# mLSTM and MoE kernel: the decay matrix from an outer product on TensorE, the last unit by halves, one more row buffer, and a new order table

## Chip, core and metric

One core of a Trainium2 chip runs the whole program. The metric is the device time of one execution in microseconds (us), the median of several runs. Of the kernel before there are three runs: 322.81, 322.91 and 323.3 us.

## What is computed

An mLSTM layer (4 batches, 8 heads, 768 steps, head size 40) is followed by a mixture-of-experts style layer (3072 tokens of width 320, hidden width 1024). Cut to what matters:

```python
for t in range(S):                       # attention part, per batch and head
    m_new = max(f[t] + m, i[t])
    f_stab = exp(f[t] + m - m_new); i_stab = exp(i[t] - m_new); m = m_new
    C = f_stab * C + i_stab * outer(v[t], k[t])
    n = f_stab * n + i_stab * k[t]
    y[t] = sigmoid(o[t]) * (C @ q[t]) / max(|n . q[t]|, 1)
x = y as (3072, 320)
h = x @ w_in                             # 320 -> 1024
e = exp(h - max(h)); solu = h * e / (sum(e) + 1e-9)
out = layer_norm(solu) * g_ln @ w_out    # 1024 -> 320
```

## The kernel before

The recurrence is computed by chunks of 128 steps. A *unit* u is one batch and one chunk, 24 units in all (6 chunks of 4 batches, chunk by chunk). First the gates of all 32 rows (batch x head) are handled at once: `m` by a scan (L393), the log decay within the chunk G by two subtractions and a scan with resets at the chunk starts (L402 to L409), and `i - m - G` on POOL (L432, L440). G goes to DRAM as the tensor `gd` (L419), and PE transposes both into `bG` (L448 to L461).

A unit then goes through these steps (names are those of the trace):

- SP loads the tokens `tk` (484 KB, v, k and q, L803) and the row `gb`: G of 8 heads x 128 steps, copied to all 128 partitions (512 KB, L804).
- DVE takes the largest magnitude `am` (L829) and its reciprocal `rr`; ACT and DVE write q and k as two float16 parts into `qs` (L849, L857); SP transposes `qs` to `qT` by DMA (L873).
- POOL sets `gb` to -1e30 above the diagonal (L889); ACT computes the decay `d` = exp(gb + bG) with 8 instructions, one per head, because the bias is another column for each (L904).
- PE computes scores into a `sy` bank of PSUM (L946), DVE multiplies them by `am` and `d` into `p` (L958), PE multiplies `p` with the values (`intra`, L1008) and adds the part of the earlier chunks (`inter`, L982, scaled on DVE as `y`, L990). DVE normalises to `x` (L1026 to L1046), POOL multiplies by the output gate (L1058). `sy` has two banks, which all of these take in turn.
- For all chunks but the last, the state is updated: POOL makes `kt` (L926), PE the state's product `upd` into the bank `sx` (L1072), DVE and POOL the new state in bfloat16 parts `cs` and `c` (L1082 to L1116), and SP copies these (L1122, L1123).
- PE transposes `x` into `sx` (L1132); ACT and DVE write high and low parts (L1137 to L1151). The first product `ph` (L1185) has 16 matmuls of 128x512. Then the softmax and norm: DVE `nm` (L1201), ACT `e` (L1208), DVE `e` again (L1234), ACT `sq` (L1243), small DVE steps up to `ab` (L1254), POOL `pw` (L1262), DVE `so` (L1266).
- ACT and POOL write `e` as two float16 parts `us` (L1287, L1277), SP transposes these by DMA into a buffer `big` (L1282), and the second product (L1305, 24 matmuls of 128x320) uses the single PSUM bank `so_`. ACT scales it to `ot` (L1321), SP writes it out (L1326).

At the start the weights come in as float64 and are decoded on ACT and DVE (L523 to L558), w_out is centred and scaled (L679, L737), and the second product can't begin before that is done. While PE waits there it runs idle matmuls (L1340).

The order of the instructions on each engine is fixed when the program is built. `Plan` takes all operations with an assumed duration each, and a list scheduler picks the next one by a rank from the table `RANK` (three numbers per step: an offset in units, one that fades over the first four units, one that grows over the last four). Each engine and each DMA queue then works strictly in that order. One rule of `Plan` matters here: operations marked `mix=1` (the steps of `intra`) are woven with one marked `mix=2` (a quarter of the second product, 6 matmuls) where both are ready, so that their matmuls alternate:

```python
if self.mix[n]:
    c = [m for m in avail[eng] if self.mix[m] == 3 - self.mix[n] and ready[m] <= s]
    if c:
        m = min(c, key=lambda m: (ops[m][5], m))
        both.append(m)
```

Of the kernel before, what the change touches and what calls it, by code (L numbers as in the profile page):

```python
# [20 lines left out]
L = 128  # L21
# [23 lines left out]
BIG = 5  # L45
# [5 lines left out]
    "sp tk": (-22.15, -15.74, 11.02),  # L51
    "sp gb": (-18.49, -14.13, -3.91),
    "sp sg": (-12.92, -3.66, 10.34),
    "act sg": (10.97, -42.22, -5.32),
    "dve am": (64.38, -5.53, 8.99),
    "dve rr": (1.15, -13.23, -1.49),
    "act qs": (0.01, 0.34, -7.27),
    "dve qs": (27.98, -124.31, 34.38),
    "sp qT": (9.36, -8.48, -13.5),
    "act dec": (3.09, 0.05, 10.84),  # L60
    "pool gb": (-8.33, 9.33, 8.59),
    "act d": (3.59, 7.99, 4.76),
    "pool kt": (16.19, 14.15, -11.51),
    "pe ps": (1.88, -8.07, -14.15),
    "dve p": (13.14, -7.12, 9.09),
    "pe sy": (-25.21, -3.11, 0.05),
    "dve y": (-9.98, -11.72, 7.82),
    "dve rd": (-12.32, 2.97, -7.38),
    "dve yi": (-11.01, -10.07, 1.66),
    "dve x": (12.24, -2.05, 6.62),  # L70
    "pool x": (-1.85, -4.93, 7.89),
    "pe sx": (1.46, -15.56, -22.4),
    "pool ct": (31.71, -5.5, -11.21),
    "dve cs": (-7.83, -3.62, -5.53),
    "pool cs": (20.95, 2.35, -4.01),
    "pool c": (11.82, 9.23, -4.49),
    "sp cs": (-5.86, -3.37, -0.69),
    "act xh": (-4.75, -11.04, 11.47),
    "dve xl": (-3.73, 2.37, -17.47),
    "pe ph": (-8.01, -14.77, -2.96),  # L80
    "dve us": (-13.91, -14.09, -14.92),
    "dve s": (-16.7, 2.43, -7.18),
    "dve nm": (-9.34, 8.77, -1.66),
    "act e": (-5.06, -11.12, 5.47),
    "dve e": (2.3, 76.54, 6.54),
    "act sq": (3.67, 47.8, 13.39),
    "dve z": (57.44, 1.42, 6.82),
    "dve ab": (-11.07, 12.82, -11.55),
    "pool pw": (-4.81, -14.34, 0.96),
    "dve so": (6.71, -4.52, 4.73),  # L90
    "act us": (13.31, 30.02, -8.95),
    "pool us": (12.85, 4.2, -8.55),
    "sp big": (7.27, -12.21, -13.1),
    "pe so_": (15.47, 4.1, 6.95),
    "act ot": (14.85, -1.73, 0.39),
    "sp ot": (13.08, -5.34, 7.83),
    "sp w_in": (-51.81,),
    "sp w_out": (-2.36,),
    "w_in": (-2.99,),
    "w_out": (-14.05,),  # L100
    "w_mul": (-13.44,),
# [232 lines left out]
def mlstm_moe_kernel(ctx: ExitStack, tc: tile.TileContext, tok, og, fg, ig, w_in, w_out, gln, out):  # L334
# [70 lines left out]
    P.op(DVE, 3330, mk_g, [G1], [F_, M_], prio=g0, port=True)  # L405
# [10 lines left out]
    for b in range(B):  # L416
        load(
            300,
            lambda P, b=b: nc.sync.dma_start(  # L419
                out=P[("gd", 0)][b].rearrange("c h l -> h c l"),  # L420
                in_=gt(P, G_)[b * H : (b + 1) * H, :].rearrange("h (c l) -> h c l", l=L),
            ),
            [("gd", 0, b)],
            [G_],
            prio=g0,
        )


    P.op(
        POOL,  # L430
        1790,
        lambda P: nc.gpsimd.tensor_tensor(out=gt(P, I_), in0=gt(P, I_), in1=gt(P, M_), op=ALU.subtract),  # L432
        [I_],
        [M_],
        prio=g0,
    )
    P.op(
        POOL,
# [947 lines left out]
```

## Time and profile before

| | |
|---|---|
| median of three runs | 322.91 us |
| profiled execution, its own time | 324.31 us |
| its span, first to last instruction | 322.5 us |
| PE, DVE, ACT, POOL busy | 279.7, 264.3, 239.7, 174.5 us |
| bytes moved by DMA | 66.66 MB |
| first matmul of a second product | 85.5 us |

The lanes are PE (matmuls), PEld (weight loads of PE), DVE, ACT, POOL and SP, which issues all DMA transfers. A row of a stage table gives its start and end, its length, busy time of each lane with the number of instructions, then the granted TensorE clock (PEclk), the mean busy share of the 16 DMA engines, and GB/s. Busy time of PE is modelled and includes idle matmuls. In a chain or a timeline the first number is the start, the second the duration. A row of waits gives the waiting engine and line, what it waited for, the total, the number of times and the longest.

### The profile page before, as it was taken

What the parts mean: (1) busy time and instruction counts of PE and PEld (TensorE: products, weight loads), DVE (VectorE), ACT (ScalarE), POOL (GpSimd) and SP (SyncE); (2) the same over time, 40 slices, a digit from 0 to 9 for tenths busy, and PEclk for the clock granted to TensorE, in tenths of its full rate; (3) what the DMA queues carried; (4) which work ended last, traced back from release to release, by engine and by line L of the source; (5) the groups of instructions that cost most, each with busy time, mean ns of one, the idle gap of its engine ahead of it and who ended that gap; (6) DMA issues with size and microseconds to landing.
All of it is one profiled execution on the core that took longest, in us unless ns stands there. A gap on an engine that the chain in (4) does not pass through costs nothing.

```text
span 322.5 us, 6918 instructions
## 1 busy us (share of the span) xinstructions
PE 279.7 (87%) x2403; PEld 229.8 (71%) x2403; DVE 264.3 (82%) x671; ACT 239.7 (74%) x505; POOL 174.5 (54%) x186
## 2 busy tenths in 40 slices
PE   0189979697989999897999969999889989999984
PEld 0189868475868888686778848878767767888753
DVE  7978998999999888859969866988889889887740
ACT  2466788989788999649979847987869967635641
POOL 6435152638467847763848655666657655434210
PEclk9999988969999999999999997999999999999999
DMA  7599995899889999999989999999998999634391
GB/s 218 202 250 252 331 255 195 196 259 224 165 255 213 238 187 231 216 250 239 217 200 227 258 208 239 185 233 225 239 200 229 212 241 190 133 66 91 82 155 58
DMA packets 118723, 66.66 MB, mean 207 GB/s; under 512 B 102880, under 2 KB 110016, under 8 KB 118688
## 3 DMA queue, kind: packets, MB, share of 16 engines
q1 hardware_dynamic: 118688, 66.21, 89.0%
q8 instruction: 19, 0.31, 0.4%
q14 instruction: 16, 0.13, 0.2%
HBM read 33.85 MB, written 4.03 MB: 117 GB/s over the span
## 4 chain that ended last, share of the span: by engine, by line
PE 42%; DVE 14%; DMA 14%; issue 13%; POOL 9%; SPq 3%; ACT 3%; POOLq 0%; ACTq 0%; DVEq 0%
PE ph L1185 14%; DMA tk<-in_tok_dram 5%; PE sy L1008 4%; DMA gb<-gd 4%; PE sx L1132 2%; DMA big<-us 2%; POOL x L1058 2%; POOL gb L889 2%; PE sy L946 2%; PE sy L982 2%; PE sx L1072 1%; POOL us L1277 1%; DVE qs L857 1%; DMA out_dram<-ot 1%; DVE wg L547 1%
## 5 line engine op out<-in xcount | busy, mean ns | idle before, releaser
L1305 PEld LDWEIGHTS <-big 128*128 128x128 f16 x576 | 63.2, 118 | 18.0 <-DMA big<-us 3.8
L904 ACT ACTIVATE d<-gb,bG 128x128 f32<-128x128 f32 x192 | 59.0, 390 | 3.5 <-POOL gb L889 1.7
L1008 PEld LDWEIGHTS sy<-tk,p 128*128 128x128 f32 x384 | 57.4, 198 | 2.9 <-DVE p L958 0.3
L849 ACT ACTIVATE qs<-tk,rr 128x640 f16<-128x640 f32 x48 | 37.2, 819 | 26.7 <-DVE rr L842 23.2
L1008 PE MATMUL sy<-tk,p 128*128 128x41 f32 x384 | 56.6, 253 | 0.1
L1277 POOL TENSOR_TENSOR us<-e,us 128x1024 f16<-128x1024 f32 x23 | 49.1, 2139 | 11.0 <-ACT us L1287 10.8
L889 POOL TENSOR_SCALAR_AFFINE_SELECT gb<-gb 128x1024 f32<-128x1024 f32 x24 | 27.3, 1137 | 37.8 <-ACT dec L885 21.7
L829 DVE TENSOR_REDUCE am<-tk 128x1 f32<-128x640 f32 x24 | 19.5, 812 | 21.9 <-DMA tk<-in_tok_dram 21.9
L958 DVE SCALAR_TENSOR_TENSOR p<-sy,am,d 128x512 f32<-128x512 f32 x48 | 35.0, 736 | 2.4 <-PE sy L946 2.3
L1262 POOL TENSOR_TENSOR pw<-ab,mhalf 128x1 f32<-128x1 f32 x24 | 13.2, 551 | 42.4 <-DVE ab L1254 41.9
L1201 DVE TENSOR_REDUCE nm<-ph 128x1 f32<-128x1024 f32 x24 | 29.2, 1217 | 7.1 <-PE ph L1185 6.9
L1185 PE MATMUL ph<-wih,xh 128*128 128x512 f32 x96 | 34.1, 437 | 0.0
L1058 POOL TENSOR_TENSOR x<-x,sg 128x320 f32<-128x320 f32 x24 | 21.8, 908 | 20.3 <-DVE rr L842 7.8
L1243 ACT ACTIVATE sq<-e,nmean 128x1024 bf16<-128x1024 f32 x24 | 27.5, 1146 | 5.8 <-DVE e L1234 5.4
L1234 DVE SCALAR_TENSOR_TENSOR e<-ph,s,e 128x1024 f32<-128x1024 f32 x24 | 30.6, 1273 | 0.9 <-ACT e L1208 0.9
L1208 ACT ACTIVATE e<-ph,nm 128x1024 f32<-128x1024 f32 x24 | 26.6, 1109 | 5.0 <-DVE nm L1201 4.7
L1185 PE MATMUL ph<-wil,xh 128*128 128x512 f32 x96 | 30.1, 394 | 0.0
L857 DVE SCALAR_TENSOR_TENSOR qs<-tk,rr,qs 128x320 f16<-128x320 f32 x48 | 29.0, 633 | 0.5 <-ACT qs L849 0.3
L1287 ACT CAST us<-e 128x1024 f16<-128x1024 f32 x24 | 24.9, 1035 | 2.7 <-issue 2.6
L1185 PE MATMUL ph<-wih,xl 128*128 128x512 f32 x96 | 26.5, 398 | 0.2 <-DVE xl L1143 0.2
L926 POOL TENSOR_TENSOR kt<-tk,d 128x320 f32<-128x320 f32 x20 | 16.5, 829 | 11.9 <-ACT d L904 10.7
L1132 PE MATMUL sx<-ident,x 128*128 128x128 f32 (+1 forms) x72 | 12.8, 289 | 10.7 <-POOL x L1058 5.9
(181 smaller groups left out, 691.7 us busy)
## 6 DMA issues: line engine op xcount, KB each, us to landing
gb<-gd SPq DMA_DIRECT2D x24, 512.0 KB
tk<-in_tok_dram SPq DMA_DIRECT2D x24, 484.0 KB
sg<-in_og_dram SPq DMA_DIRECT2D x12, 320.0 KB
out_dram<-ot SPq DMA_DIRECT2D x24, 160.0 KB
big<-in_w_out_dram SPq DMA_DIRECT2D x4, 640.0 KB
cs<-cs SPq DMA_DIRECT2D x20, 102.5 KB
big<-in_w_in_dram SPq DMA_DIRECT2D x4, 512.0 KB
cs<-c SPq DMA_DIRECT2D x20, 51.2 KB
```

Source lines behind the costliest of these rows:

```text
L849: nc.scalar.activation(out=dst, in_=q_src(P, a).unsqueeze(2).to_broadcast([L, H, 2, D]), func=AF.Copy, scale=P[rr],)
L857: V.scalar_tensor_tensor(out=q_parts(P, a, 2 - a, 1), in0=q_src(P, a), scalar=P[rr], in1=q_parts(P, a, 0, 1), op0=ALU.mult, op1=ALU.subtract,)
L889: lambda P: nc.gpsimd.affine_select(out=P[gb], in_=P[gb], pattern=[[0, H], [1, L]], base=0, channel_multiplier=-1, compare_op=ALU.is_ge, f ...
L904: nc.scalar.activation(out=P[d_t][:, h, :], in_=P[gb][:, h, :], func=AF.Exp, bias=P[BG][:, 0, c, b * H + h : b * H + h + 1],)
L958: lambda P, j=j, ps=ps: V.scalar_tensor_tensor(out=P[p_t][:, 4 * j : 4 * j + 4, :], in0=P[ps].rearrange("p (h l) -> p h l", l=L), scalar=P ...
L1008: nc.tensor.matmul(yv(P)[:, h, :], lhsT=P[p_t][:, h, :], rhs=v1(P)[:, h, :], start=True, stop=True)
L1058: lambda P: nc.gpsimd.tensor_tensor(out=P[x], in0=P[x], in1=P[sg][:, u % OG, :], op=ALU.mult),
L1185: nc.tensor.matmul(P[ph][:, j * 512 : (j + 1) * 512], lhsT=a, rhs=w[:, j * 512 : (j + 1) * 512], start=n == 0, stop=n == 7,)
L1201: lambda P: V.tensor_reduce(out=P[nm], in_=P[ph], axis=AX.X, op=ALU.max, negate=True),
L1234: lambda P: V.scalar_tensor_tensor(out=P[e], in0=P[ph], scalar=P[sc], in1=P[e], op0=ALU.mult, op1=ALU.mult, accum_out=P[nmean]),
L1277: (V if last else nc.gpsimd).tensor_tensor(out=P[us[1]][:, 1], in0=P[e], in1=P[us[0]][:, 0], op=ALU.subtract)
L1305: nc.tensor.matmul(P[po][:, 0:DM], lhsT=uTv(P, a)[:, k, :], rhs=P[w][:, k, :], start=n == 0, stop=n == 23)
```

## The change

Seven things are done together.

1. The decay comes from TensorE. `i - m - G` (b) and G are split into two parts (rounded to the matmul format, and the rest) and go to DRAM as `bd` and `gd`. For each unit SP loads 16 rows of 128 into `el` (b's parts for 8 heads) and 2 x 8 x 128 into `er` (G's parts). Rows 0 and 1 of `el` are ones, the other rows of `er` say which head a row is for, the rest is zero. One matmul over all 128 rows makes the exponents of four heads in a `sy` bank; ACT takes exp of 512 columns at once (2 instructions in place of 8); POOL sets `d` to zero above the diagonal afterwards, in place of `gb` beforehand; DVE multiplies the scores into `d` itself, so that `p` is gone and `d` has 3 buffers.
2. The 512 KB load `gb` and the buffers `gb` and `p` are gone.
3. `kt` takes the last column of `d` from a small copy `dl` that ACT makes. The decay of the state comes for all units at once from one matmul at the start (`sel`, `dec`) in place of 16 small ACT steps.
4. The gates' steps on POOL move to DVE, and four small steps split the parts.
5. The state's product `upd` is marked `mix=1` with 8 steps: it may be woven into the second product.
6. The last unit goes by halves of 512 columns: first product, maximum, exp, multiplication, float16 parts, four transposes of half the size, second product by halves.
7. `BIG` is 6 in place of 5, and all numbers of `RANK` are others.

```diff
-BIG = 5
+BIG = 6
 RANK = {
-    "sp tk": (-22.15, -15.74, 11.02),
+    "sp tk": (-18.64, 10.68, -13.3),
...
-        load(1500, lambda P: nc.sync.dma_start(out=P[gb], in_=P[("gd", 0)][b, c].partition_broadcast(L)), [gb], [("gd", 0, b)], prio=rank(SPQ, "gb"))
+        load(
+            100,
+            lambda P: nc.sync.dma_start(
+                out=P[el].bitcast(F32)[2 : 2 + 2 * H],
+                in_=P[BD].rearrange("p a s -> (p a) s")[b * 2 * H : (b + 1) * 2 * H, c * L : (c + 1) * L],
+            ),
...
+        load(
+            100,
+            lambda P: nc.sync.dma_start(
+                out=P[er].bitcast(F32)[0:2],
+                in_=P[GD][b * H : (b + 1) * H, :, c * L : (c + 1) * L].rearrange("h a l -> a h l"),
+            ),
...
-        def decay(P, j):
-            for h in range(4 * j, 4 * j + 4):
-                nc.scalar.activation(
-                    out=P[d_t][:, h, :],
-                    in_=P[gb][:, h, :],
-                    func=AF.Exp,
-                    bias=P[BG][:, 0, c, b * H + h : b * H + h + 1],
-                )
+        for j in range(2):
+            pd = ("sy", ("d", u, j))
+
+            def exponents(P, j=j, pd=pd):
+                nc.tensor.matmul(
+                    P[pd],
+                    lhsT=P[el],
+                    rhs=P[er].rearrange("p h l -> p (h l)")[:, j * 512 : (j + 1) * 512],
+                    start=True,
+                    stop=True,
+                )
+
+            P.op(PE, 232, exponents, [pd], [el, er], rank(PE, "d"))
+            op(
+                ACT,
+                600,
+                lambda P, j=j, pd=pd: nc.scalar.activation(
+                    out=P[d_t][:, 4 * j : 4 * j + 4, :],
+                    in_=P[pd].rearrange("p (h l) -> p h l", l=L),
+                    func=AF.Exp,
+                ),
+                [(*d_t, j)],
+                [pd],
+            )
...
-            op(PE, 700, upd, [pu], [kt, tk])
+            op(PE, 750, Steps(H, upd), [pu], [kt, tk], mix=1)
...
+        if last:
+            for j in range(2):
+                op(PE, 1864, lambda P, j=j: first(P, range(8), (j,)), [(*ph, j)], [xh, xl, (*x3, 0), (*x3, 1), *w_k[0], *w_k[1], *w_2])
```

How the change moves instructions, at the places that the prediction speaks of. PE, a unit in the middle of the kernel. Before, from the end of the first product (L1185) over the state's product (L1072) to the scores (L946) and the next second product (L1305):

```order
1483 L1185 MATMUL ph<-wih,x_2903 128x512 x2
1484 L1185 MATMUL ph<-wil,x_2903 128x512 x2
1485 L1072 MATMUL sx<-tk,kt 40x41 x8
1486 L946 LDWEIGHTS qT
1487 L946 MATMUL sy<-qT 128x128
```

The same place after the change; L1014 is the exponents' product (names `er` and `el`), L1326 the first product, L1085 the scores:

```order
1537 L1148 MATMUL sy<-tk,d 128x41 x4
1538 L1014 MATMUL sy<-er_97,el_106 128x512
1539 L1326 MATMUL ph<-wih,xh 128x512 x2
1540 L1326 MATMUL ph<-wil,xh 128x512 x2
1541 L1326 MATMUL ph<-wih,xh 128x512 x2
1542 L1326 MATMUL ph<-wil,xh 128x512 x2
1543 L1326 MATMUL ph<-wih,xl 128x512 x4
1544 L1014 MATMUL sy<-er_97,el_106 128x512
1545 L1326 MATMUL ph<-wih,x_2848 128x512 x2
1546 L1326 MATMUL ph<-wil,x_2848 128x512 x2
1547 L1085 LDWEIGHTS qT
1548 L1085 MATMUL sy<-qT 128x128
```

The two exponents' products stand around the first product, and the block of 8 matmuls of the state's product is gone from there. It now stands here, woven with the second product (L1530):

```order
1563 L1210 MATMUL sx<-tk,kt 40x41
1564 L1530 LDWEIGHTS big
1565 L1530 MATMUL so__2978<-woh,big 128x320
1566 L1210 MATMUL sx<-tk,kt 40x41
1567 L1530 LDWEIGHTS big
1568 L1530 MATMUL so__2978<-wol,big 128x320
1569 L1210 MATMUL sx<-tk,kt 40x41
1570 L1530 LDWEIGHTS big
1571 L1530 MATMUL so__2978<-woh,big 128x320
1572 L1210 MATMUL sx<-tk,kt 40x41 x2
```

In all, 112 of the 160 state's matmuls stand beside one of the second product, where 2 did before; of the 192 of `intra` 125 do, where 149 did before. Of the 48 exponents' products 11 stand ahead of the first second product and 37 behind it.

SP, the queue of the DMA transfers, two units in the middle. Before (L803 tokens, L1282 and L873 transposes, L1122 and L1123 copies of the state, L804 `gb`, L1326 output):

```order
110 L803 DMA tk<-in_tok_dram 128x968
111 L1282 DMA_TRANSPOSE big<-us 128x16x128
112 L1122 DMA cs_2513<-cs_2513 40x656
113 L1123 DMA cs_2513<-c_2583 40x328
114 L804 DMA gb<-gd 128x1024
115 L873 DMA_TRANSPOSE qT<-qs_81 128x16x128
116 L1326 DMA out_dram<-ot 128x320
```

After (L910 tokens, L1493 and L999 transposes, L913 `el`, L923 `er`, L1557 output):

```order
141 L1493 DMA_TRANSPOSE big<-us 128x16x128
142 L910 DMA tk<-in_tok_dram 128x968
143 L913 DMA el_109<-bd 16x128
144 L999 DMA_TRANSPOSE qT<-qs_68 128x16x128
145 L1262 DMA cs_2825<-cs_2825 40x656
146 L1263 DMA cs_2825<-c_2885 40x328
147 L1557 DMA out_dram<-ot 128x320
148 L923 DMA er_103<-gd 2x8x128
```

The load of 512 KB is gone, two of 8 KB stand in its place, and the tokens are still asked for next to a transpose of `us`.

DVE, the first steps. Before (L393 and L409 scans, L402 and L403 subtractions, L531 and L547 decoding of weights):

```order
3 L393 SCALAR_TENSOR_TENSOR p<-p,us 32x768
4 L402 TENSOR_TENSOR d<-p 32x767
5 L403 TENSOR_TENSOR d<-d,p 32x767
6 L531 TENSOR_SCALAR e<-uc 128x512
7 L409 SCALAR_TENSOR_TENSOR us<-d 32x768
```

After (L435 and L444 make b, L460 the two rests, L649 and L660 decode weights):

```order
12 L444 TENSOR_TENSOR us<-us 32x768
13 L558 COPY dec<-so__151 40x192
14 L633 TENSOR_SCALAR e<-uc 128x512
15 L963 TENSOR_SCALAR am<-am 128x1
16 L983 SCALAR_TENSOR_TENSOR qs_68<-tk,rr,qs_68 128x8x40
17 L968 RECIPROCAL rr<-am 128x1
18 L649 SCALAR_TENSOR_TENSOR e<-big,e 128x512
19 L460 TENSOR_TENSOR us<-us,d 32x768
20 L660 SCALAR_TENSOR_TENSOR e<-big,e 128x512
21 L460 TENSOR_TENSOR us<-us,d 32x768
```

Four more passes over the gates stand on DVE, among the decoding of the first weights.

More of the change, by code (lines that the diff above doesn't have):

```diff
@@ L415, in mlstm_moe_kernel @@
     )
[L416 to L425, printed above, removed]
-        )
     P.op(
-        POOL,
-        1790,
-        lambda P: nc.gpsimd.tensor_tensor(out=gt(P, I_), in0=gt(P, I_), in1=gt(P, M_), op=ALU.subtract),
+        DVE,
+        870,
+        lambda P: V.tensor_tensor(out=gt(P, I_), in0=gt(P, I_), in1=gt(P, M_), op=ALU.subtract),
         [I_],
@@ new lines, in first @@
+        def first(P, ns, js):
+            for n in ns:
+                a, w = terms[n](P)
+                for j in js:
+                    nc.tensor.matmul(
+                        P[ph][:, j * HF : (j + 1) * HF],
+                        lhsT=a,
+                        rhs=w[:, j * HF : (j + 1) * HF],
+                        start=n == 0,
+                        stop=n == 7,
+                    )
+        if last:
+            for j in range(2):
+                op(PE, 1864, lambda P, j=j: first(P, range(8), (j,)), [(*ph, j)], [xh, xl, (*x3, 0), (*x3, 1), *w_k[0], *w_k[1], *w_2])
+        else:
+            for g in range(4):
+                op(PE, 932, lambda P, g=g: first(P, (2 * g, 2 * g + 1), (0, 1)), [ph], first_in[g])
@@ L1251, in unit, with squares @@
+        def squares():
+            op(
+                ACT,
+                1135,
+                lambda P: nc.scalar.activation(
+                    out=P[sq], in_=P[e], func=AF.Square, bias=P[nmean], scale=-float(DFF), accum_out=P[su]
+                ),
+                [sq, su],
+                [*([(*e, 0), (*e, 1)] if last else [e]), nmean],
+            )
+        squares()
         small(lambda P: V.tensor_scalar(out=P[z], in0=P[z], scalar1=1.0e-9, scalar2=EPS_Z, op0=ALU.add, op1=ALU.mult), z)
@@ L1307, in second @@
+        for g, some in enumerate(pairs):
+            def second(P, i, g=g, some=some):
+                a, w, k = some[i]
+                nc.tensor.matmul(
+                    P[po][:, 0:DM],
+                    lhsT=uTv(P, a)[:, k, :],
+                    rhs=P[w][:, k, :],
+                    start=g == 0 and i == 0,
+                    stop=g == 3 and i == len(some) - 1,
                 )
-            some = pairs[6 * g : 6 * g + 6]
             op(
                 PE,
-                820,
-                Steps(6, second),
+                20 + 134 * len(some),
+                Steps(len(some), second),
@@ L1314, in unit @@
                 [po],
-                [*{uT[a] for a, _, _ in some}, *{(*w, k // 2) for _, w, k in some}],
+                [
+                    *({(*uT[a], k // 4) for a, _, k in some} if last else [uT[0]]),
+                    *{(*w, k // 2) for _, w, k in some},
+                ],
                 mix=2,
```

497 lines of the change are left out of this document (329 added, 168 removed).

## Prediction

> **What bounds the kernel now.** I read the page's head first, then a table by stages. I cut the stages at the first second product (85.5 us), at the end of the token loads (261.9 us), and where the last first products begin (291.2 us). Two shorter tables follow. The first head line is the span; the stage rows give start and end, length, busy time of PE, PEld, DVE, ACT and POOL, the granted clock, the DMA share and GB/s.
>
> ```profile
> span 322.5 us, 6918 instructions
> core 0: us, PE busy (x) PEld busy (x) DVE busy (x) ACT busy (x) POOL busy (x), PEclk, DMA share, GB/s
> 0.00:85.50 85.50, 61.99 (x448) 53.56 (x449) 77.67 (x155) 64.35 (x138) 39.34 (x45) 0.94 0.87 232
> 85.50:261.90 176.40, 162.37 (x1520) 132.43 (x1519) 146.51 (x407) 142.18 (x302) 113.48 (x123) 0.99 1.01 223
> 261.90:291.20 29.30, 29.30 (x270) 24.46 (x269) 25.83 (x71) 19.98 (x44) 14.99 (x13) 1.00 0.70 148
> 291.20:322.50 31.30, 26.04 (x173) 19.31 (x171) 14.32 (x41) 13.22 (x24) 6.69 (x6) 1.00 0.50 100
> ...
> 191.60:204.40 12.80, 12.00 (x100) 9.55 (x101) 9.58 (x27) 10.30 (x21) 9.19 (x11) 0.87 1.04 223
> 204.40:214.60 10.20, 10.20 (x103) 8.59 (x100) 8.83 (x27) 9.26 (x21) 5.07 (x7) 1.00 1.09 219
> ```
>
> Up to 85.5 us DVE carries the work (77.67 of 85.5). From there to 261.9 us PE is busy 162.37 of 176.4 us, so it idles 14.0 us, while the DMA share is 1.01. In the next stage the large loads are over, the share falls to 0.70, and PE doesn't idle at all. A unit that waits for nothing takes 10.2 us (the last row). In the row above, the same number of matmuls took 12.0 us of PE time at a granted clock of 0.87: a stall costs a little clock too.
>
> Why PE idles, the waits and the chain of work show. The first three rows are waits of the whole span, the fourth is one of PE from 85.5 to 291.2 us; the rest is a piece of the chain.
>
> ```profile
> POOL pw L1262 <- DVE ab L1254: 41.9, 17, 6.3
> DVE am L829 <- DMA tk<-in_tok_dram: 21.9, 13, 3.8
> PE sy L946 <- DVE x L1046: 3.3, 2, 1.8
> ...
> PE sx L1132 <- POOL x L1058: 4.8, 6, 1.3
> ```
>
> ```profile
> 123.87 4.07 DMA out_dram<-ot
> ...
> 137.54 2.87 SPq L1282
> ...
> 140.51 3.93 DMA tk<-in_tok_dram
> ...
> 144.46 0.82 DVE am L829
> ```
>
> SP hands a transpose of `us` to the DMA queues for 2.87 us, only then asks for the tokens, and these take 3.93 us. DVE stands at `am` for them, 13 times and 21.9 us in all. Behind `am` on DVE stand `ab` and `x`; POOL waits 41.9 us for `ab` at `pw`, and PE for POOL's `x`. So the stalls of PE in the middle begin at late tokens, and the DMA is full there.
>
> **The change, part by part.** The sum is made against the profiled execution's own 324.31 us (span 322.5, and 1.81 around it). The median of the runs, 322.91, lies 1.40 below it.
>
> *DMA.* The next rows are the two largest loads and SP's time to issue one `gb`.
>
> ```profile
> gb<-gd SPq DMA_DIRECT2D x24, 512.0 KB
> tk<-in_tok_dram SPq DMA_DIRECT2D x24, 484.0 KB
> ...
> L804 SPq DMA_DIRECT2D gb<-gd x24: 347/426/1432, 12.4 to 260.6; - x24
> ```
>
> `gb` is 24 x 0.524 = 12.6 MB. In the middle stage 176.4 us at a share of 1.01 serve 16 units, 11.1 us each; 223 GB/s at 1.01 is 221 GB/s for a full share, so one `gb` takes about 2.4 us of it. Without it a unit needs some 8.7 us, below PE's 10.2, and the two small loads add at most a part of that. SP gets one issue more per unit, about 0.43 us; the transposes, `cs` and output queued behind it shift by that. I take 11 of the 14.0 us of stalls as gone, since in the stage with a share of 0.70 none is left; the bounds are 0 and all 14.0. With the stalls goes most of the clock loss (12.0 against 10.2 to 10.5 us): 1.2, bounds 0 to 1.5.
>
> Against this speaks that a transfer's landing isn't in proportion to its size: 160 KB of output took 4.07 us in the chain, the 484 KB of tokens 3.93. If the small loads cost the DMA what the large one did, nothing is freed; that is the first rival. The Trainium skill, "DMA: Bandwidth & Descriptors", section "Rules for kernel authors", says so as a rule: transfers under 64 KB are mostly overhead and should be joined. By its table two transfers of 4 KB would take about 1.4 us as an estimate, so the relief would be nearer 1 than 2.4 us. No run here shows an 8 KB load yet.
>
> *PE.* The prices are from the chain: the first product, the state's product, an `intra` alone (4 heads) and woven (one head), and a second product.
>
> ```profile
> 95.35 0.15 PE sy L1008 x2
> 95.50 0.14 PE so__1029 L1305
> 95.63 0.82 PE sy L1008 x8
> ...
> 199.51 3.74 PE ph L1185 x16
> 203.25 0.74 PE sx L1072 x16
> ```
>
> A matmul of 512 columns takes 3.74/16 = 0.234 us. The exponents' products are of this form; 37 come behind 85.5 us, so +8.7 us on the engine that then bounds; the 11 earlier ones stand where PE runs idle matmuls. `intra` costs 0.205 us a head alone (0.82/4) and 0.15 woven. It is woven for 24 heads fewer: 24 x 0.055 = +1.3. The state's product costs 0.74/8 = 0.0925 a head alone; woven it isn't in the trace. If it shrinks as `intra` does (0.15/0.205), to 0.068, 112 heads save 2.8 us. Bounds: half hidden, -5.2, or as dear as a woven `intra`, 0.0575 x 112 = +6.4. I take -2.8, since its columns are the same 41 and its weights fewer. PE's sum is +7.2.
>
> *ACT.* The first row is the old exp (192, union of busy time 59.0), the second the nearest of 512 columns.
>
> ```profile
> L904 ACT ACTIVATE d<-gb,bG 128x128 f32<-128x128 f32 x192 | 59.0, 390 | 3.5 <-POOL gb L889 1.7 <-DVE s L1229 0.8 <-DVE z L1251 0.7
> L523 ACT ACTIVATE uc<-big 128x512 f32<-128x512 f32 x5 | 3.3, 662 | 8.2 <-DMA big<-in_w_in_dram 8.2
> ```
>
> 59.0 us become 48 x 0.66 = 32 and 20 small copies in place of 16 small exps. ACT was busy 142 of 176 us and bounds nothing alone: no gain of its own, only shorter queues.
>
> *POOL and DVE in the middle.* The select has the same size and moves behind the exp; DVE's multiplication is the same. Nothing, as long as the exponents are computed early enough; the order has them around the first product of an earlier unit.
>
> *The start.* These rows are DVE's first steps.
>
> ```profile
> 1.01 0.91 DVE L782 MEMSET qs<- 128x1024 uint32 x1 [1.01 <-PEq L1377]
> ...
> 3.45 1.75 DVE L393 TENSOR_TENSOR_SCAN p<-p,us 32x768 f32<-32x768 f32 x1 [0.45 <-DMA us<-in_ig_dram]
> 5.22 0.94 DVE L402 TENSOR_TENSOR d<-p 32x767 f32<-32x767 f32 x1
> 6.20 2.44 DVE L403 TENSOR_TENSOR d<-d,p 32x767 f32<-32x767 f32 x1
> ...
> 16.61 0.55 DVE L458 COPY bG<-so__138 128x384 f32<-128x384 f32 x1
> ...
> 23.33 1.41 DVE L958 SCALAR_TENSOR_TENSOR p<-sy,am,d 128x512 f32<-128x512 f32 x2 [1.59 <-PE sy L946]
> ```
>
> Four passes over the gates are added (4 x 0.94 = 3.8) and a small copy replaces a small copy. L403 may fall from 2.44 to 0.94 as its twin L402, if POOL's step beside it was what slowed it (-1.5). The smaller memsets are worth nothing, since DVE waits for the gates until 3.45 us. That is +2.3, of 7.8 us that DVE idles before 85.5 us. I take +1. The bounds are +3.5 (the first scores' product, now at 23.33, moves to about 27, since two stores and two loads follow the last pass) and -3 (the freed DMA and ACT take away some of the idle time).
>
> *The end.* The chain from 299.9 us on is the last first product, then four second products, each behind an `ot` that empties the one bank.
>
> ```profile
> 299.90 3.80 PE ph L1185 x16
> 303.70 3.29 PE so__4386 L1305 x24
> 306.99 0.02 issue
> 307.01 0.54 ACT ot L1321
> 307.55 0.04 issue
> 307.59 3.43 PE so__4437 L1305 x24
> ```
>
> The new order puts one of the four ahead of the last first product, so one gap of 0.6 us (306.99 to 307.59) hides behind it: -0.6. Then only two products, 2 x (3.43 + 0.6) = 8.1 us, cover the last unit's chain. Halves let it start a second product's first quarter earlier; if they didn't, about 1.5 us would come back, so the bounds are -0.6 and +1.5. The sixth `big` buffer: PE never waited long for it; nothing.
>
> *Sum.* 324.31 + 1 + 8.7 + 1.3 - 2.8 - 0.6 - 11 - 1.2 = 319.7, and less 1.40 the median is **318.3**.
>
> **Rivals.**
>
> - *The late tokens stay (slower).* SP's order still sets the tokens next to a transpose of `us`, with `ab` and `x` behind `am` on DVE. If the stalls come from this order or from each transfer's fixed time, not from bytes, all 14.0 us stay: 324.31 + 1 + 7.2 - 0.6 - 1.40 = 330.5. For it speaks the 4.07 us for 160 KB; against it the stage at 0.70 without a stall. It decides from where less than 7.6 us of stalls and clock are saved (1 + 7.2 - 0.6).
> - *The banks of `sy` (slower).* Two banks now serve six uses a unit, not four, and a bank of exponents is held until ACT has come to its exp. PE waited 1.65 us each of 2 times for a bank that DVE's `x` held. If this comes in one unit of three behind 85.5 us, 6 x 1.65 = 10 us more: 328.3.
> - *Half the relief.* If stalls and clock give back 7.6 us where I take 12.2, the added work eats it up and it comes out even: 322.9. The share that stays near 1.01 x 8.7/11.1 at the old pace, and higher at a faster one, speaks for some stalls to stay.
> - *Everything goes (faster).* All 14.0 us and 1.5 of clock go, and the start gains 3: 324.31 - 3 + 7.2 - 0.6 - 15.5 - 1.40 = 311.0.
>
> **How the numbers follow.** The forecast has 0.54; with its own unknowns (start, woven price, stalls of 8 to 13) it spans about 314 to 322. Everything goes 0.18, even 0.09, late tokens 0.13, banks 0.06. A measurement of this kernel tells 0.2% (0.65 us) from no change. Faster: 0.54 + 0.18 = 0.72; same 0.09; slower 0.13 + 0.06 = 0.19. The range goes from the end of the fast case, 311, to 325.5: above it lie the two slower rivals' values, so a little under 2 in 10 are left out.
>
> **What would show it.** Right: no `gb`, a DMA share near 0.9 in the middle, `am` waiting for tokens well under 21.9 us, PE idle there under 5 us, a unit at about 10.6 us, 512-column exponents at 0.23 us on PE, exp near 0.66 us on ACT, the first second product near 86.5 us, and `ot` three times between the last second products. Wrong: the wait of `am` as long as before, waits of L1014 or L1085 for ACT or DVE, woven state's matmuls above 0.1 us a head, or a first second product past 89 us.

## The result and the profile after

The changed kernel takes 339.43 us (median of four runs, 337.77 to 340.31), the kernel before 323.11 beside it. The ratio is 1.0483, with a 95% interval of 1.0418 to 1.0547: 4.8% slower, where 318.3 us was forecast, and above the range. Now and then an execution runs slower at a lower granted clock: medians here are over all runs, ratios leave such runs out and go by the runs of the kernel before on the same occasion (medians 322.17 to 323.17 us), and stage columns are empty where the profile fell on one.

The stages of the changed kernel, cut at its first second product (78.5 us), in the middle, and where the last unit's work begins (the columns are those of the first table of the prediction):

```profile
core 0: us, PE busy (x) PEld busy (x) DVE busy (x) ACT busy (x) POOL busy (x), PEclk, DMA share, GB/s
0.00:78.50 78.50, 63.63 (x493) 54.17 (x494) 70.23 (x149) 54.40 (x95) 32.68 (x47) 1.00 0.77 205
78.50:270.00 191.50, 187.93 (x1543) 145.16 (x1543) 162.48 (x415) 126.27 (x215) 118.57 (x126) 0.99 0.76 166
270.00:311.00 41.00, 39.97 (x335) 32.07 (x335) 34.81 (x91) 24.68 (x43) 18.31 (x17) 1.00 0.52 108
311.00:337.30 26.30, 19.76 (x120) 13.27 (x117) 9.74 (x30) 9.96 (x20) 3.92 (x4) 0.94 0.40 91
```

The start is 7.0 us shorter (78.5, was 85.5), which was not forecast; in the middle PE idles only 3.6 of 191.5 us, which was (under 5), at a DMA share of 0.76. Yet from the first second product to the end there are 337.3 - 78.5 = 258.8 us, where before there were 322.5 - 85.5 = 237.0. PE is busy all the time and gets less done. Its waits say the same (the waits of the whole span):

```profile
DVE cs L1234 <- PE sx L1210: 20.0, 14, 1.5
...
PE sy L1085 <- DVE x L1186: 3.5, 4, 1.0
...
DVE am L955 <- DMA tk<-in_tok_dram: 1.6, 2, 1.2
```

The late tokens are gone (1.6 us, were 21.9). New is a wait of DVE for PE, 14 times 1.4 us: 14 is the number of units whose state's product is woven. The group of that product, and one such place in PE's timeline (start, duration, line; `x2` stands for the two passes of one head, `x4` for two heads):

```profile
L1210 PE MATMUL sx<-tk,kt 128*40 128x41 f32 x320 | 32.5, 214 | 0.4 <-POOL kt L1065 0.4
```

```profile
204.87 0.27 PE L1210 MATMUL sx<-tk,kt 128*40 128x41 f32 x2
205.07 0.31 PE L1530 MATMUL so__2789<-woh,big 128*128 128x320 f16 x1
205.31 0.27 PE L1210 MATMUL sx<-tk,kt 128*40 128x41 f32 x2
205.52 0.31 PE L1530 MATMUL so__2789<-wol,big 128*128 128x320 f16 x1
...
206.20 0.35 PE L1210 MATMUL sx<-tk,kt 128*40 128x41 f32 x4
206.48 0.31 PE L1530 MATMUL so__2789<-wol,big 128*128 128x320 f16 x1
...
207.80 0.31 PE L1530 MATMUL so__2789<-woh,big 128*128 128x320 f16 x1
...
209.77 0.57 PE L1122 MATMUL sy<-cs,qT 120*128 120x41 bf16 x16
210.18 0.30 PE L1530 MATMUL so__2789<-woh,big 128*128 128x320 f16 x1
210.31 0.31 PE L1148 MATMUL sy<-tk,d 128*128 128x41 f32 x2
210.45 0.31 PE L1530 MATMUL so__2789<-woh,big 128*128 128x320 f16 x1
```

The distances between starts are what to read, since the durations overlap. A head of the state's product and a second matmul take 0.44 us together (204.87 to 205.31); by the prediction's rows they take 0.0925 + 0.137 = 0.23 apart (0.74/8 and 3.29/24). Both distances are longer: 0.20 us from the head to the second matmul, 0.24 back. Where two heads stand side by side, the second adds only 0.08 us (206.20 to 206.48 is 0.28). A second matmul and a woven `intra` a few rows on take 0.27 together (210.18 to 210.45), without such a surcharge. `128*40` and `128*128` are the weights, rows by columns: `intra` has the shape of the second product's weights, the state's product has 40 columns.

### The profile page after: what moved, and what is told of

The parts are those of the page before. It is cut to its first block, busy times and chain, and to the rows that moved or that the text cites. A ratio compares the mean times of both kernels' runs of the same rounds, so it can differ in the third digit from the quotient of the medians.

```text
span 337.3 us, 6976 instructions
## 1 busy us (share of the span) xinstructions
PE 311.3 (92%) x2485; PEld 244.7 (73%) x2485; DVE 277.3 (82%) x682; ACT 215.3 (64%) x372; POOL 173.5 (51%) x193
## 5 line engine op out<-in xcount | busy, mean ns | idle before, releaser
L1530 PEld LDWEIGHTS <-big 128*128 128x128 f16 x576 | 61.8, 115 | 21.4 <-issue 6.0
L1148 PEld LDWEIGHTS sy<-tk,d 128*128 128x128 f32 x384 | 53.8, 192 | 3.4 <-issue 0.8
L1148 PE MATMUL sy<-tk,d 128*128 128x41 f32 x384 | 53.2, 252 | 0.6 <-DVE d L1097 0.4
L1040 POOL TENSOR_SCALAR_AFFINE_SELECT d<-d 128x1024 f32<-128x1024 f32 x24 | 29.1, 1212 | 35.5 <-ACT dl L1036 32.3
L983 DVE SCALAR_TENSOR_TENSOR qs<-tk,rr,qs 128x320 f16<-128x320 f32 x48 | 39.5, 841 | 0.8 <-ACT qs L975 0.5
L1097 DVE SCALAR_TENSOR_TENSOR d<-sy,am,d 128x512 f32<-128x512 f32 x48 | 34.7, 739 | 1.6 <-PE sy L1085 1.2
L1026 ACT ACTIVATE d<-sy 128x512 f32<-128x512 f32 x48 | 28.1, 590 | 8.8 <-PE sy L1014 8.5
L1210 PE MATMUL sx<-tk,kt 128*40 128x41 f32 x320 | 32.5, 214 | 0.4 <-POOL kt L1065 0.4
L1247 POOL TENSOR_TENSOR cs<-cs 40x328 f32<-40x328 f32 x20 | 14.8, 740 | 34.7 <-DVE cs L1234 22.1
L1326 PE MATMUL ph<-wih,xh 128*128 128x512 f32 x96 | 31.7, 408 | 0.6 <-ACT xh L1278 0.6
L1210 PEld LDWEIGHTS sx<-tk,kt 128*40 128x40 f32 x320 | 20.1, 116 | 15.4 <-issue 1.1
L1326 PE MATMUL ph<-wil,xh 128*128 128x512 f32 x96 | 30.3, 393 | 0.0
L1326 PE MATMUL ph<-wih,xl 128*128 128x512 f32 x96 | 26.9, 400 | 0.6 <-DVE xl L1283 0.6
L1234 DVE TENSOR_TENSOR cs<-ct,sx 40x328 f32<-40x328 f32 x16 | 7.8, 488 | 20.1 <-PE sx L1210 20.0
```

Of the source, the lines that this page charges most:

```text
L983: V.scalar_tensor_tensor(out=q_parts(P, a, 2 - a, 1), in0=q_src(P, a), scalar=P[rr], in1=q_parts(P, a, 0, 1), op0=ALU.mult, op1=ALU.subtract,)
L1026: lambda P, j=j, pd=pd: nc.scalar.activation(out=P[d_t][:, 4 * j : 4 * j + 4, :], in_=P[pd].rearrange("p (h l) -> p h l", l=L), func=AF.Exp,),
L1040: lambda P: nc.gpsimd.affine_select(out=P[d_t], in_=P[d_t], pattern=[[0, H], [1, L]], base=0, channel_multiplier=-1, compare_op=ALU.is_ge, ...
L1097: lambda P, j=j, ps=ps: V.scalar_tensor_tensor(out=P[p_t][:, 4 * j : 4 * j + 4, :], in0=P[ps].rearrange("p (h l) -> p h l", l=L), scalar=P ...
L1148: nc.tensor.matmul(yv(P)[:, h, :], lhsT=P[p_t][:, h, :], rhs=v1(P)[:, h, :], start=True, stop=True)
L1210: nc.tensor.matmul(P[pu][0:D, h * E1 : (h + 1) * E1], lhsT=P[kt][:, h, :], rhs=v1(P)[:, h, :], start=True, stop=True)
```

## The experiments

**The theory.** PE doesn't hide a change between narrow and full weights; weaving makes 14 such changes per unit (one into the first head, 13 behind it) where a block has two. **Rivals:** the loss lies in the exponents' product and its chain, or in the new order; or weaving costs whatever the width. The first four kernels separate these. "Rest" is the time from the first second product to the end of the profiled execution.

| kernel | median, us | ratio to before (95%) | first second product, us | rest, us |
|---|---|---|---|---|
| before | 323.11 | | 85.5 | 237.0 |
| after | 339.43 | 1.0483 (1.0418 to 1.0547) | 78.5 | 258.8 |
| after, block | 319.34 | 0.9886 (0.9823 to 0.9949) | 80.1 | 237.8 |
| after, planner's own block | 321.41 | 0.9943 (0.9902 to 0.9983) | | |
| before, woven | 342.74 | 1.0608 (1.0527 to 1.0689) | 85.2 | 254.7 |
| woven, 64 columns | 344.24 | 1.0685 (1.0608 to 1.0762) | 82.3 | 261.7 |
| woven, 80 columns | 322.33 | 1.0011 (0.9977 to 1.0045) | 80.3 | 239.4 |
| woven, 128 columns | 333.06 | 1.0316 (1.0251 to 1.0381) | 84.0 | 247.0 |
| block, exponents over 18 rows | 330.37 | 1.0227 (1.0158 to 1.0296) | 82.0 | 246.8 |
| before, 64 KB loads | 317.90 | 0.9854 (0.9796 to 0.9913) | 90.2 | 225.7 |
| block, large load back | 363.27 | 1.1228 (1.1153 to 1.1303) | | |
| block, five row buffers | 318.71 | 0.9851 (0.9790 to 0.9912) | 79.5 | 238.2 |
| block, no halves | 318.67 | 0.9834 (0.9768 to 0.9901) | 80.7 | 235.3 |
| block, other order in the tail | 320.05 | 0.9886 (0.9833 to 0.9940) | 81.2 | 238.0 |

### The block in the woven place

```diff
-                steps = [((i + 0.5) / f.n, i, f) for f in (a, b) for i in range(f.n)]
+                steps = [
+                    ((i + 0.5) / f.n if f.step.__name__ != "upd" else -1.0, i, f) for f in (a, b) for i in range(f.n)
+                ]
```

> The changed kernel with its order of work on every engine kept, except that the eight matmuls of the state's product run as a block ahead of the second product's six, not woven into them (112 heads, 14 units). Theory (weaving 40-column f32 weights into the second product is what costs): a woven pair took 0.44 us where 0.0925 + 0.137 = 0.23 apart, so 14 units x some 1.4 to 1.65 us come back: 339.4 - 19 to 23 = 316 to 320 us, and the woven matmuls' gaps vanish from the profile. Rival A (the exponents' product and its chain, or the new order of the table, makes the unit 12.4 us long): within 2 us of 339.4. Rival B (part of the loss comes back as stalls, since the engines beside TensorE had no pressure at the slow pace): 324 to 333 us, TensorE waiting by over 8 us more than in the changed kernel.

Measured: 319.34 us, 20.1 less than the changed kernel, with nothing else moved. The same place in its timeline of PE:

```profile
206.64 0.81 PE L1212 MATMUL sx<-tk,kt 128*40 128x41 f32 x16
207.39 0.31 PE L1532 MATMUL so__2978<-woh,big 128*128 128x320 f16 x1
207.53 0.30 PE L1532 MATMUL so__2978<-wol,big 128*128 128x320 f16 x1
```

Eight heads take 0.75 us (206.64 to 207.39), and six second matmuls at 0.137 us another 0.82: 1.57 us. Woven, from the first head to the second matmul behind the eighth, there are eight heads and the six second matmuls between them, 207.80 - 204.87 = 2.93; 13 of the 14 woven places in this trace take 2.92 or 2.93. 14 units x 1.36 = 19.0 us of the 21.0 by which the rests differ. (The expectations below say seven matmuls and 1.71 us; that counted the matmul at which the distance ends.) The other 2.0 us are of the size of PE's longer waits for `x`: 3.5 us woven, 0.6 and 0.4 as a block. Both rivals fall: the rest of the change is no loss, and nothing comes back as stalls.

### The block where the planner puts it

```diff
-            op(PE, 750, Steps(H, upd), [pu], [kt, tk], mix=1)
+            op(PE, 700, lambda P: [upd(P, h) for h in range(H)], [pu], [kt, tk])
```

> The changed kernel with the state's product as one block that the planner places by itself, not joined to the second product; the intra product then stands woven for 92 and not 116 single matmuls, and the order of other rows shifts. Theory: 315 to 322 us, within 3 us of the run with the block at the woven place; it is the whole change without the weaving. Rival A: within 3 us of 339.4. If it is 4 us or more above the block at the woven place, the order that the table sets is worth that much by itself.

Measured: 321.41 us. It is the whole change without the weaving, and 2.1 us above the run before; 92 single heads of `intra` are woven in place of 116, which by the prediction's 0.055 us would be 1.3. The intervals overlap, so more can't be read from it.

### The kernel before, with the weaving alone

```diff
-            op(PE, 700, upd, [pu], [kt, tk])
+            op(PE, 750, Steps(H, upd), [pu], [kt, tk], mix=1)
```

> The kernel before with one part of the change alone: the state's product of 14 units (112 heads) woven into the second product by the same rule; the planner then weaves 96 and not 149 single matmuls of the intra product, and moves other rows by little. Theory (weaving costs 1.4 to 1.65 us a unit on TensorE): the kernel before waits for transfers for some of its time, so part is hidden: 323.1 + 10 to 24 = 333 to 347 us. Rival A (the loss comes from the exponents' product or the new order): 322 to 326 us.

Measured: 342.74 us, 20.5 more than the kernel before beside it (322.23). That is within the theory's range, and the rival falls: the weaving alone makes the kernel before slower, by as much as it makes the changed one. That the two numbers are alike is in part chance. A woven place takes 2.92 or 2.93 us here too (12 of 14), but in the rest PE idles 11.3 us where it idled 19.3, so that part of the surcharge fills old stalls, and `intra`, woven for 53 heads fewer, is 5.3 us dearer (26.8 against 21.5 us from start to start).

### The width of the woven weights

The woven order stays, only the number of columns per head changes (here 128; the 64 and 80 differ in the two numbers).

```diff
-    tag("kt", [L, H, D], F32, 2)
+    tag("kt", [L, H * D + L - D], F32, 2)
...
-                    P[pu][0:D, h * E1 : (h + 1) * E1], lhsT=P[kt][:, h, :], rhs=v1(P)[:, h, :], start=True, stop=True
+                    P[pu][:, h * E1 : (h + 1) * E1], lhsT=P[kt][:, h * D : h * D + L], rhs=v1(P)[:, h, :], start=True, stop=True
```

> The changed kernel with the state's product still woven, in the same order, but its weights 128 columns wide: each head loads its own 40 columns and the 88 that follow them (88 zeros behind the last head); the 88 rows of the result more are not read. A memset of 88 columns per unit comes onto GpSimd. Theory 1 (a change of the weights' width, 40 to 128 columns and back, is what TensorE cannot hide): woven pairs fall from 0.44 to some 0.24 to 0.30 us, 316 to 325 us. Theory 2 (the cost is the weaving of f32 weights into f16 weights, or of two matmuls of this size, whatever the width): pairs stay at 0.40 us or more, 335 to 343 us; the woven intra product (f32 moving part against the same f16 second product, 0.15 us a pass) speaks against it. Rival A (the loss lies elsewhere): 337 to 341 us with pairs of any length.

Measured: 333.06 us; the pairs went to 0.29 us as theory 1 said, the time only a third of the way, above theory 1's range. Its timeline of PE, eight heads and six second matmuls from the first row to the start of the last:

```profile
204.63 0.37 PE L1213 MATMUL sx<-tk,kt 128*128 128x41 f32 x2
204.82 0.31 PE L1533 MATMUL so__2804<-woh,big 128*128 128x320 f16 x1
204.97 0.31 PE L1213 MATMUL sx<-tk,kt 128*128 128x41 f32 x2
205.11 0.31 PE L1533 MATMUL so__2804<-wol,big 128*128 128x320 f16 x1
...
206.76 0.31 PE L1533 MATMUL so__2804<-woh,big 128*128 128x320 f16 x1
```

2.13 us are 0.80 less than with 40 columns: the distances are 0.14 to 0.15 us both ways. But a head with 128 columns costs more by itself. In the units whose product isn't woven, eight of them take 1.70 us as a block, where eight with 40 took 0.74. I had left that price out. To part the two, 64 and 80 columns:

> The changed kernel, state's product woven, weights 64 columns wide (a head's 40 and the next 24). Eight woven heads with seven matmuls of the second product between them took 2.93 us with 40 columns and 2.13 us with 128; block and second product apart take 1.71 us. Theory T (the array is used in halves or whole, and a switch between these is not hidden): 64 columns still pay, 2.8 to 3.1 us a unit, 336 to 341 us. Theory N (the cost falls evenly with the number of columns): about 2.7 us, 336 us. Theory F (only under 64 columns cost): 1.8 to 2.0 us, 322 to 328 us.

> As the run with 64 columns, with 80 (a head's 40 and the next 40). Theory T (anything beyond 64 columns is the whole array): 1.8 to 2.2 us for eight heads and seven second matmuls, 326 to 334 us, as with 128. Theory S (any width but 128 pays): 2.8 to 3.1 us, 336 to 341 us. Theory N: about 2.5 us, 334 us.

Measured: 344.24 us with 64 columns, 322.33 with 80. First the timeline with 64, then that with 80; in each the first row is the first head, the last row the second matmul behind the eighth.

```profile
198.22 0.31 PE L1213 MATMUL sx<-tk,kt 128*64 128x41 f32 x2
198.47 0.31 PE L1533 MATMUL so__2634<-woh,big 128*128 128x320 f16 x1
198.71 0.31 PE L1213 MATMUL sx<-tk,kt 128*64 128x41 f32 x2
...
201.47 0.31 PE L1533 MATMUL so__2634<-woh,big 128*128 128x320 f16 x1
```

```profile
207.55 0.29 PE L1213 MATMUL sx<-tk,kt 128*80 128x41 f32 x2
207.67 0.31 PE L1533 MATMUL so__2994<-woh,big 128*128 128x320 f16 x1
207.82 0.27 PE L1213 MATMUL sx<-tk,kt 128*80 128x41 f32 x2
...
209.28 0.31 PE L1533 MATMUL so__2994<-woh,big 128*128 128x320 f16 x1
```

3.25 us with 64 columns, 1.73 with 80. Each of these runs also has units whose product stands as a block, so each width can be set beside its own block (the shortest distance that eight heads take as a block, and six second matmuls at 0.137 us):

| columns | block of eight heads, us | apart, us | woven, us | surcharge, us |
|---|---|---|---|---|
| 40 | 0.75 | 1.57 | 2.93 | 1.36 |
| 64 | 1.06 | 1.88 | 3.25 | 1.37 |
| 80 | 1.10 | 1.92 | 1.73 | -0.19 |
| 128 | 1.70 | 2.52 | 2.13 | -0.39 |

The surcharge doesn't shrink with the columns, it ends between 64 and 80. That is where theory T has it, though its times missed: 344.24 us is above its range, 322.33 below. That PE works in another shape of the array up to 64 columns is theory T's explanation; the runs show the boundary, not the shape. Beyond the boundary the weaving does gain against a block of the same width, as the prediction hoped. But no wider weave comes below the 1.57 us of the narrow block: with 80 columns it is 1.73.

### The rows of the weights

```diff
-                    lhsT=P[el],
-                    rhs=P[er].rearrange("p h l -> p (h l)")[:, j * 512 : (j + 1) * 512],
+                    lhsT=P[el][0 : 2 + 2 * H],
+                    rhs=P[er][0 : 2 + 2 * H].rearrange("p h l -> p (h l)")[:, j * 512 : (j + 1) * 512],
```

> The changed kernel with the state's product as a block, and the exponents' product over the 18 rows that hold something, not over 128 (110 rows of zeros and of ones against zeros are left out; the same result). Order unchanged. Theory 1 (what TensorE cannot hide is any change in the weights' shape, rows too): two switches of 0.1 us for each of 37 products between full-size neighbours, 319.3 + 4 to 8 = 323 to 327 us, the products at 0.42 us or more. Theory 2 (only the number of columns matters): 318 to 320.5 us, products at 0.22 to 0.32 us as now.

Measured: 330.37 us, 11.0 above the block with 128 rows, more than I had put down. A product between two first products, here with 18 rows and then, from the block's run, with 128:

```profile
190.06 1.09 PE L1328 MATMUL ph<-wih,xl 128*128 128x512 f32 x4
191.09 0.49 PE L1016 MATMUL sy<-er,el 18*128 18x512 f32 x1
191.51 0.73 PE L1328 MATMUL ph<-wih,x 128*128 128x512 f32 x2
192.08 0.63 PE L1328 MATMUL ph<-wil,x 128*128 128x512 f32 x2
```

```profile
203.99 1.10 PE L1328 MATMUL ph<-wih,xl 128*128 128x512 f32 x4
204.92 0.39 PE L1016 MATMUL sy<-er,el 128*128 128x512 f32 x1
205.15 0.63 PE L1328 MATMUL ph<-wih,x 128*128 128x512 f32 x2
205.62 0.62 PE L1328 MATMUL ph<-wil,x 128*128 128x512 f32 x2
```

From the first row's start to the last row's start, 2.02 us against 1.63: 0.39 us for one product with 18 rows in this place. 37 products behind the start would give 14 us, but behind `intra` or a second product, where the one with 128 rows takes 0.32 or 0.34 us itself, it is less: added from start to start over the rest, the exponents' products, the first products and `intra` take 122.6 us with 18 rows and 112.2 with 128, 0.28 for each of the 37. The rest grew by 9.0, since the block's second products were 1.3 us slower (12 of them at its end take 0.267 us each, at a lower granted clock). So a change of rows costs too, here 0.39 us for the way there and back, and the 110 rows of zeros are what keep the exponents' product cheap. 120 and 80 rows do not pay: in the timeline of the changed kernel above, the 16 products of `inter` (half of them 120 rows, half 80) take 0.41 us together.

### The bytes

First, the kernel before with a 64 KB load in place of the 512 KB; the select and the small exponentials read that tile for all heads.

```diff
-        load(1500, lambda P: nc.sync.dma_start(out=P[gb], in_=P[("gd", 0)][b, c].partition_broadcast(L)), [gb], [("gd", 0, b)], prio=rank(SPQ, "gb"))
+            one[0] = sb.tile([L, 1, L], F32, name="g1", tag="g1", bufs=2)
+            nc.sync.dma_start(out=one[0], in_=P[("gd", 0)][b, c, 0:1].partition_broadcast(L))
...
-                in_=P[gb],
+                in_=one[0].to_broadcast([L, H, L]),
```

> The kernel before with one thing changed: the broadcast load of the gates brings one head's row (64 KB) and not eight (512 KB) per unit, and the select and the old exponentials use that row for all heads (the other seven heads' gates are left out). Same count of loads, same order on every engine, 11 MB less moved. Theory 1 (bytes held TensorE's stalls and the slow start): of 14.0 us of stalls, 1.2 us of clock and 5 to 7 us of the start most goes, 323.1 - 9 to 20 = 303 to 314 us, waits for tokens near 5 us. Theory 2 (each transfer's own time, or the order on SP and DVE, held them; eight times fewer bytes in the same 24 loads change little): 320 to 325 us, tokens waited for as before.

Measured: 317.90 us, a ratio of 0.9854, between the ranges of the two theories. Its stages, cut at its first second product, and its wait for tokens:

```profile
0.00:90.20 90.20, 63.15 (x448) 53.92 (x449) 82.79 (x158) 64.95 (x140) 38.82 (x45) 0.91 0.68 179
90.20:315.90 225.70, 214.48 (x1958) 175.51 (x1956) 185.21 (x513) 174.31 (x366) 134.25 (x141) 1.00 0.84 175
```

```profile
DVE am L835 <- DMA tk<-in_tok_dram: 9.5, 8, 1.8
```

The rest is 225.7 us, 11.3 less than before, and PE idles 11.2 us of it where it idled 19.3: that is the relief, in the place where the prediction had it. The start is not shorter but 4.7 us longer, at a granted clock of 0.91 (0.94 before), so half of theory 1 falls: bytes held the stalls, not the start. Why the start is longer was not traced.

Second, the block with five row buffers and the large load back, behind `er`:

```diff
+                nc.sync.dma_start(
+                    out=sb.tile([L, H, L], F32, name="gx", tag="gx", bufs=1),
+                    in_=P[GD][b * H : (b + 1) * H, 0, c * L : (c + 1) * L].partition_broadcast(L),
+                ),
```

> The same with five row buffers and, behind each unit's load of the exponents' rows, the 512 KB broadcast load that the change took out, into a tile that nobody reads: the bytes of the kernel before are back (12.6 MB more), the order of every engine is the same. To be set beside the run with five buffers. Theory 1 (fewer bytes are what took TensorE's stalls away and brought the first second product forward by 5 us): the DMA share goes to about 1.0 in the middle, waits for tokens and transposed rows return, 5 to 14 us more, 324 to 334 us. Theory 2 (the new order and ScalarE's shorter exponentials took the stalls away, the bytes did not matter): within 2 us of the run with five buffers.

Measured: 363.27 us, 44.6 more than the run with five buffers and beyond both theories. The load stands behind the unit's small loads, in an order of SP that had no place for it:

```profile
DVE am L963 <- DMA tk<-in_tok_dram: 29.9, 13, 4.7
...
PE sy L1093 <- DMA qT<-qs: 7.2, 2, 6.6
```

Tokens are waited for 29.9 us, the transposed queries 7.2 (in an execution of 369.52 us, so a part of that is not the load's). But the DMA share from 90 to 330 us is only 0.88, where theory 1 put 1.0. That points at the load's place in the queue more than at its bytes; the two were not parted. It is no measure of the relief, since the order of before was made with such a load in it.

### The buffer, the halves, the tail

```diff
-BIG = 6
+BIG = 5
```

> The changed kernel with the state's product as a block (the run of 319.3 us), and five row buffers in place of six, the order of every engine the same. Theory (transfers have slack now, TensorE is busy nearly throughout): 318.5 to 321 us, no difference that can be measured. Rival (the sixth buffer is what keeps the transposed rows early): 322 to 327 us, with waits of the second product for its rows.

Measured: 318.71 us. The sixth buffer is worth nothing that can be measured.

```diff
-        last = u == NU - 1
+        last = False
```

> The changed kernel with the state's product as a block, and the last unit whole, not by halves of columns (the planner then orders the last 25 us as it sees fit: the last first product goes ahead of one second product more, 23 rows of TensorE's order move). Theory (the halves win little, since second products cover the chain and the eviction queued behind the halves' casts costs 1.9 us): within 1.5 us of 319.3. Rival (the halves are worth the quarter product's start that they were costed with): 320.5 to 322 us.

Measured: 318.67 us. From the start of the matmul behind the last first product to the end of the span there are 19.3 us with halves (298.6 to 317.9), 18.8 without (297.2 to 316.0), and 19.0 in the kernel before (303.5 to 322.5). The halves win nothing that can be measured.

```diff
-                op(ACT, 520, lambda P, sl=sl: nc.scalar.copy(out=P[us[0]][:, 0, sl], in_=P[e][:, sl]), [(*us[0], j)], [(*e, j)])
+                op(ACT, 520, lambda P, sl=sl: nc.scalar.copy(out=P[us[0]][:, 0, sl], in_=P[e][:, sl]), [(*us[0], j)], [(*e, j)], behind=[("ot", NU - 3)])
```

> The changed kernel with the state's product as a block, and in the last unit ScalarE evicts the third-last unit's result before it casts the two halves of the last unit's rows, not behind them (two rows of its order change places). TensorE waits 2.45 us for that eviction now, 0.5 to 0.6 us behind earlier ones. Theory (the tail's path runs through it): 1.5 to 2 us less, 317.3 to 317.8 us. Rival (the casts, 0.5 us later, then hold the next second product's rows, or the granted clock takes it back): 318.8 to 319.8 us.

Measured: 320.05 us, no gain. The planner put the casts behind the squares too (they begin 3.7 us after the last exponential where it was 1.6), so it is no clean trial of the theory, and PE's waits changed places. First the block's row, then that of the new order:

```profile
PE so__4415 L1532 <- ACT ot L1554: 2.4, 1, 2.4
```

```profile
PE so__4452 L1532 <- DMA big<-us: 3.0, 3, 1.8
```

## Why the prediction was wrong, step by step

**The step that failed** is the price of the woven state's product: "I take -2.8, since its columns are the same 41 and its weights fewer." Fewer weights are what makes it dear. The term measured +20.1 us (339.43 against 319.34), outside its own bounds of -5.2 to +6.4. The lower end was half the block's own price, the upper that of a woven `intra`, whose weights are full. Neither came from a row with a 40-column product between second matmuls: the trace of before held it as a block, where the one switch behind it hides in 0.74 us for eight heads. The prediction named the right sign of error ("woven state's matmuls above 0.1 us a head"), but had no rival that priced it.

The timelines show the surcharge: 14 units x 1.36 us. From the first head on, a woven place has 13 switches and the block one behind it, so a switch costs 1.36 / 12 = 0.11 us. The rows fit: a head by itself is 0.08 us, and 8 x 0.08 + 0.11 is the block's 0.75. A rule that speaks against this change stands in the Trainium skill, "TensorEngine Tiling (Array Packing)", section "Key Properties": changing the tiling mode drains TensorE. Its section "Available Configurations" lists 128x64 and 32x128 beside 128x128. The runs agree: 40 and 64 columns and 18 rows pay, 80 columns and 80 or 120 rows do not. That the switch is such a change of mode is inferred from this boundary, not seen in a trace. The prediction did not weigh this rule.

The other terms, in profiled time:

| term | predicted, us | measured, us | by |
|---|---|---|---|
| start | +1 | -7.0 (-5.4 in the block) | first second product |
| woven state's product | -2.8 | +20.1 | after against block |
| stalls and clock in the middle | -12.2 | -11.3 | rest with 64 KB loads |
| exponents, `intra`, tail | +8.7 + 1.3 - 0.6 = +9.4 | +12.1 | rest of the block, 237.8 - 225.7 |

- **Stalls and clock** were right, in size and in cause, as far as a load of 64 KB stands for two of 8 KB. How much DMA time two 8 KB loads in place of the large one free, the main queue's rows say (packets, MB, share of 16 engines' span), first of the kernel before, then of the block:

```profile
q1 hardware_dynamic: 118688, 66.21, 89.0%
```

```profile
q1 hardware_dynamic: 116464, 54.32, 75.9%
```

  89.0% of 322.5 us less 75.9% of 317.9 are 45.7 us, in 24 units 1.9 us each: between the two values of the prediction, 2.4 and 1. The rule behind the lower one (the Trainium skill, "DMA: Bandwidth & Descriptors", section "Rules for kernel authors") points the right way, but the page's table makes the two loads too dear: an estimate of 1.4 us by it, where 2.4 - 1.9 leaves about 0.5.
- **Exponents:** an exponents' product is 0.23 us between first products (204.92 to 205.15), 0.32 behind `intra` (212.40 to 212.72 in the changed kernel) and 0.34 behind a second product, where 0.234 was taken throughout. There are 17, 9 and 11 of these, 10.5 us. `intra` takes 23.3 us of the rest from start to start where the kernel with 64 KB loads has 21.4, so +1.9 where 1.3 was taken. Together that is the 12.1.
- **The start** had the wrong sign. It is not the bytes (90.2 us with 64 KB loads) and not the weaving (85.2 and 80.1). DVE carries the start, and its steps that split the weights, of the same shapes, ran faster. Two of their groups before 85.5 us in the kernel before, then the same two before 78.5 us in the changed one:

```profile
L547 DVE SCALAR_TENSOR_TENSOR e<-big,e 128x512 int32<-128x512 int32 x5 | 6.2, 1242 | 0.1
L547 DVE SCALAR_TENSOR_TENSOR wg<-big,wg 128x640 int32<-128x640 int32 x4 | 4.1, 1033 | 0.0
```

```profile
L649 DVE SCALAR_TENSOR_TENSOR e<-big,e 128x512 int32<-128x512 int32 x5 | 3.4, 678 | 0.0
L649 DVE SCALAR_TENSOR_TENSOR wg<-big,wg 128x640 int32<-128x640 int32 x4 | 3.3, 821 | 0.1
```

  These two give 3.6 us, three more such groups 1.7, and L403's twin fell to 0.945 us as the prediction thought it might (1.5). I had priced what is added on DVE and not what its old steps would gain. Against it stand the four added passes (3.7) and the scan behind them (2.58 us, where L409 took 1.74), so these parts leave some 2.2 of the 7.0 us; the rest stays open. The runs with the old start show 1242 and 1241 ns again (the woven one and that with 64 KB loads), those with the new one 677 to 679; yet the first second product comes between 78.5 and 84.0 us in these. What slows the steps, the timelines of DVE and POOL before show:

```profile
30.64 1.93 DVE L547 SCALAR_TENSOR_TENSOR e<-big,e 128x512 int32<-128x512 int32 x1
31.16 0.85 POOL L1058 TENSOR_TENSOR x<-x,sg 128x320 f32<-128x320 f32 x1
39.71 0.69 DVE L547 SCALAR_TENSOR_TENSOR e<-big,e 128x512 int32<-128x512 int32 x1
```

  The five steps L547 on `e` take 1.67, 0.69, 1.23, 1.93 and 0.69 us. The three long ones begin beside a step of POOL and end about 0.55 us after one ends (here 30.64 + 1.93 = 32.57 and 31.16 + 0.85 = 32.01); the two short ones have none beside them. After the change POOL has no step beside any of the five, and each takes 0.66 to 0.69 us. By these timelines POOL's steps hold these steps of DVE; a run without them was not made.
- **The tail and the sixth buffer:** nothing, as forecast within its bounds.
- **The rivals:** the banks of `sy` don't hold (PE waits 3.5 us for `x`, where 10 were priced), and the late tokens are gone. The result is slower for a reason that no rival named. Without the failed term, the sum stood at 321.1; the block measured 319.34. That they lie so near is partly luck: in the block the start was 6.4 us better than priced, the last two terms together 3.6 worse.

## What to carry to other kernels

Before weaving small matmuls into large ones, compare the shapes of the weights: narrow weights (up to 64 columns here) between full ones cost two switches of 0.11 us each, and belong in one block; widening to 80 columns removes the switch, but the narrow block stays cheaper (1.57 against 1.73 us). A product with 18 rows among ones with 128 was worth padding with zeros to the full height. And a price for an operation in a new neighbourhood needs a row with that neighbourhood in it, or bounds that allow for a switch.

## What the runs showed of the hardware

- The end of the surcharge between 64 and 80 columns: 3.25 against 1.73 us for the same eight heads and six second matmuls, and nearly the same surcharge with 40 and 64 columns, 1.36 and 1.37 us.
- 18 rows in place of 128 made the kernel 11.0 us slower, 0.39 us for a product between two first products, though the other 110 rows are zeros.
- The profile counts PE as busy through the switches: the woven kernel's PE was busy for 187.93 of 191.5 us while its rest was 21.0 us longer than the block's. Distances between starts in the timeline show it, the busy time does not.
- A step of DVE on 128x512 int32 took 0.69 us, and 1.23 to 1.93 beside steps of POOL.
